# Other places for the staged output projection, eight attention-output buffers, and a shifted plan in block 0

## The chip, the cores and the metric

The kernel runs on one core of one Trainium2 chip. The metric is the device time of one execution in microseconds; lower is better. A program of this kind has five engines: TensorE (PE, whose weight loads are shown as PEld), VectorE (DVE), ScalarE (ACT), GpSimd (POOL) and SyncE (SP). Each works through its own queue in order. TensorE writes its results to PSUM, which has eight banks here; the other engines read them from there into SBUF. DMAs are issued from the queues of SP, ACT and POOL.

## The reference

A token sequence of 2048 rows with 576 columns goes through a layer norm, and the result feeds two branches that are multiplied at the end:

```python
xn = _layernorm(x)
# branch A: attention with 32 query heads on a cache of 16 key/value heads,
#           of which only the last W = 512 positions count
q = (xn @ wq) as 32 heads of 128
p = softmax(q @ k^T * 128 ** -0.5);  o = p @ v
s = concat_heads(o) @ wo                      # 4096 -> 576
# branch B: a token mixer and an MLP
h  = gelu(_layernorm(xn) @ w1)                # 576 -> 576
hs = concat(four column groups of h, shifted by +1, -1, +2, -2 tokens) @ w2
x1 = xn + hs
b  = x1 + gelu(_layernorm(x1) @ w3) @ w4      # 576 -> 4608 -> 576
out = x + s * silu(b)
```

All tensors are bf16.

## The kernel before

**Two stages.** The tokens are cut into four blocks of 512 (`NB` = 4, `TB` = 4 tiles of 128 tokens each). Stage one does branch A for all blocks, with the mixer of branch B woven in; it leaves `s` and `x1` in DRAM (`s_dram`, `x1_dram`). Stage two does the MLP and the final product. Its SBUF pools begin at the place where those of stage one began, so its weights `w3_s`, `w3r_s`, `w4_s` (nine slices of four 128-column chunks, loaded on SP by `load_w`) fall on space that stage one used; each tile waits for the tiles that it covers.

**The loop over heads.** Stage one runs over `U` = 128 heads, 32 per block, and some more steps for the last block's remainder. Step `u` issues on TensorE, in this order: the first quarter of head `u`'s scores (`stage_s`, L403), the query projection of head `u + 1` (`stage_q`, L388), and then the other three quarters of the scores, each followed by a piece of other work: half of head `u - 1`'s product with the values (`stage_v`, L420) after each of the first two, and a third of the step's fill atoms after each of the three. At the end of the step, `stage_t` (L433) issues the transpose of head `u - 1`'s output on SP.

The path of one head: `psq` in PSUM is copied to `qT` (by VectorE at L393 in block 0, by ScalarE at L395 later); scores `sc` become `pT` by an exponential on ScalarE (L405); `po` in PSUM holds two token tiles of output with the row sums in an extra column; VectorE takes the reciprocal (L424) and multiplies into `o` (L425); a DMA transpose on SP turns `o` into `oT`. So a buffer of `o` is held from the first L425 of its head until the transpose has read it. There are four `o` buffers, two `po` banks, three `qT`, ten `pT` and 36 `oT`.

**Work that fills the heads.** Lists give the step at which each other piece is issued: `pe(u, atoms)` for matmuls, which are cut in three parts over the step, and `at(u, fn)` or `later(u, ...)` for the rest. `later` with 3 issues nine steps of a layer norm, three in each head. For a block `b` with `base = 32 * b`, before the change:

- `ln2_steps` from `base + 7`: the second layer norm, into `xnn_b`; `tr2` at `base + 10` to `+13`: four DMA transposes on SP into `xnnT` (L357).
- `b1` (L492): five matmul groups for `w1` from `xnnT`, with the GELU on VectorE and ScalarE (`gelu1`), from `base + 17` in block 0.
- `b2` and `b2_rem` (L543) of the block before, from `base + 21`, whose sum with `xn` goes to an `x1` tile and by SP to `x1_dram` (L570). Its tile is taken one head earlier (`b2_shift`).
- `ln1_steps` for the next block (bn_stats at L133, L134, the inverse root by Newton steps, applied at L144), from head 20 in block 0 and from `base + 24` later; `tr1`: its four transposes on SP into `xT_b` (L357), at heads 23 to 26 in block 0. The next block's `stage_q` reads them.
- `wo_atoms` of the block before: the output projection in five groups, four of 32 wide matmuls (512 columns) and one remainder group of 128 narrow ones (64 columns), at heads `base + 1` to `base + 5`. Each wide group is copied from PSUM by ScalarE (L454), the remainder at L461; then a DMA stores the block to `s_dram` (L462). Block 3's groups come after the last head, and its store is issued by ScalarE; the others by SP.
- Weight loads on GpSimd: `load_wq`, `load_wo`, `load_k`, `load_v`, several of them held back by `late` until a chosen head's `pT` exists.

SP, POOL and PE issue strictly in this written order in stage one. The order on VectorE and ScalarE is made by the framework's scheduler; the instructions under `tc.high_priority` (the copies of `qT` and `kT`, L424, L425, the GELU) are preferred, and the layer norms fill what is left. SP's queue is thus one line in which `stage_t`, `tr1`, `tr2` and the stores stand one behind the other.

**The staging of s, and x1_pool.** Before, `s` is staged in a pool of its own, `so_pool`, with one buffer. `x1_pool` has two buffers, which hold in turn: the staged keys (`load_k`, read last by `prep_k` in head 27), block 0's and block 1's x1, block 0's x1 read back for the MLP (`load_x1(0)`, head 106), and then block 2's and block 3's x1. `w1_sb` is read last by `b1` of block 3, at head 117.

Of the kernel before, what the change touches and what calls it, by code (L numbers as in the profile page):

```python
# [8 lines left out]
P = 128  # L9
# [3 lines left out]
BF16 = mybir.dt.bfloat16  # L13
# [18 lines left out]
def kernel(  # L32
# [18 lines left out]
    _, S, D = A_x.shape  # L51
# [11 lines left out]
    NB = S // QB  # L63
    TB = QB // P
# [31 lines left out]
    def rows(ap, t0, n):  # L96
        return ap[t0 * P:(t0 + n) * P, :].rearrange("(tt p) d -> p tt d", p=P)
# [98 lines left out]
    x1_pool = ctx.enter_context(tc.tile_pool(name="x1_pool", bufs=2))  # L196
# [19 lines left out]
    with ExitStack() as actx:  # L216
        def pool(name, bufs, space=None):
            kw = {} if space is None else {"space": space}
            return actx.enter_context(tc.tile_pool(name=name, bufs=bufs, **kw))
# [7 lines left out]
        w1_sb = res.tile([P, NDC, D], BF16, name="w1_sb")  # L227
# [6 lines left out]
        xraw = pool("xraw", 4)  # L234
        qT_pool = pool("qT_pool", 3)
        pT_pool = pool("pT_pool", 10)
        o_pool = pool("o_pool", 4)
        hb_pool = pool("hb_pool", 2)
        hs_pool = pool("hs_pool", 1)
        g1_pool = pool("g1_pool", 1)  # L240
        so_pool = pool("so_pool", 1)
        oT_pool = pool("oT_pool", 36)
        wo_sb = pool("a_wo", 1).tile([P, Hq, D], BF16, name="wo_sb")

# [8 lines left out]
        def load_x(b, eng):  # L253
            x_t[b] = []
            for tt in range(TB):
                xt = xraw.tile([P, D], BF16, name="xt")
                t = b * TB + tt
                eng.dma_start(out=xt[:], in_=x2[t * P:(t + 1) * P, :])
                x_t[b].append(xt)
# [43 lines left out]
        def late(ap, fn):  # L303
            g = nc.gpsimd.tensor_copy(out=gate[:, :], in_=ap)
            with tc.issue_after(g.ins):
                fn()
# [49 lines left out]
        def transpose_tile(dstT, src, tt):  # L356
            nc.sync.dma_start(out=dstT[:, :, tt * P:(tt + 1) * P], in_=src[:, tt, :], transpose=True)  # L357
# [14 lines left out]
        def tr1(b, tt):  # L372
            transpose_tile(xT_b[b % 2], xn_t[b], tt)
# [62 lines left out]
        so_t = {}  # L436

        def wo_atoms(qb):
            psp, tag = (ps_pq, "pq") if qb == NB - 1 else (ps_wo, "wo")
            groups = []  # L440
            st = {}

            def mm(ps, h, tt, lo, hi):
                nc.tensor.matmul(ps, lhsT=oT_t[qb * Hq + h][:, tt, :], rhs=wo_sb[:, h, lo:hi], start=(h == 0),  # L444
                                 stop=(h == Hq - 1))

            def main(tt, h):
                if tt == 0 and h == 0:
                    so_t[qb] = so_pool.tile([P, TB, D], BF16, name="s_out")
                if h == 0:  # L450
                    st["ps"] = psp.tile([P, M0], FP32, name="pswo", tag=tag)
                mm(st["ps"][:, :], h, tt, 0, M0)
                if h == Hq - 1:
                    nc.scalar.activation(out=so_t[qb][:, tt, 0:M0], in_=st["ps"][:, :], func=ACT.Copy, scale=0.5)  # L454

            def rem(tt, h):
                if tt == 0 and h == 0:
                    st["pr"] = psp.tile([P, TB, R0], FP32, name="pswr", tag=tag)
                mm(st["pr"][:, tt, :], h, tt, M0, D)
                if tt == TB - 1 and h == Hq - 1:  # L460
                    nc.scalar.activation(out=so_t[qb][:, :, M0:D], in_=st["pr"][:, :, :], func=ACT.Copy, scale=0.5)  # L461
                    (nc.scalar if qb == NB - 1 else nc.sync).dma_start(out=rows(s_dram, qb * TB, TB),  # L462
                                                                       in_=so_t.pop(qb)[:])

            for tt in range(TB):
                groups.append([lambda tt=tt, h=h: main(tt, h) for h in range(Hq)])
            groups.append([lambda tt=tt, h=h: rem(tt, h) for tt in range(TB) for h in range(Hq)])
            return groups

# [3 lines left out]
        def ln2_steps(b):  # L473
            return layernorm_steps(small, [xnn_b[:, tt, 0:D] for tt in range(TB)],
                                   [xn_t[b][:, tt, 0:D] for tt in range(TB)])

        def tr2(b, tt):
            transpose_tile(xnnT, xnn_b, tt)

        def b1(b, c):  # L480
            st = {}

            def mm(kc):
                if kc == 0:
                    if c == 0:
                        hb_t[b] = hb_pool.tile([P, 5, QB + 2 * PAD], BF16, name="hb")
                        if b == 0:
                            nc.vector.memset(hb_t[b][:, :, 0:PAD], 0.0)
                        if b == NB - 1:
                            nc.vector.memset(hb_t[b][:, :, PAD + QB:], 0.0)  # L490
                    st["ph"] = ps_pq.tile([P, QB], FP32, name="ph", tag="pq")
                nc.tensor.matmul(st["ph"][:, :], rhs=xnnT[:, kc, :],  # L492
                                 lhsT=w1r_sb[:, kc, :] if c == 4 else w1_sb[:, kc, c * c4:c * c4 + P],
                                 start=(kc == 0), stop=(kc == NDC - 1))
                if kc == NDC - 1:
                    gelu1(b, c, st["ph"])

            return [lambda kc=kc: mm(kc) for kc in range(NDC)]
# [25 lines left out]
        def b2_shift(b):  # L524
            with tc.high_priority(offset=HP):
                b2_shift_(b)
# [18 lines left out]
        def b2(b, tt):  # L545
            st = {}

            def mm(c):
                if c == 0:
                    st["ps"] = ps_wo.tile([P, M0], FP32, name="psx1", tag="wo")  # L550
                b2_mm(st["ps"][:, :], b, tt, c, 0, M0)
                if c == 4:
                    with tc.high_priority(offset=HP):
                        nc.vector.tensor_tensor(out=x1o_t[b][:, tt, 0:M0], in0=st["ps"][:, :],
                                                in1=xn_t[b][:, tt, 0:M0], op=ALU.add)

            return [lambda c=c: mm(c) for c in range(5)]
# [38 lines left out]
        def at(u, fn):  # L596
            fill.setdefault(u, []).append(fn)

        def pe(u, atoms):
            pe_fill.setdefault(u, []).extend(atoms)  # L600
# [5 lines left out]
        def later(u, make, per):  # L606
            cell = []
            for i in range(2 * TB + 1):
                def step(i=i):
                    if not cell:  # L610
                        cell.append(make())
                    cell[0][i]()
                at(u + i // per, step)

        for b in range(NB):
            base = b * Hq
            if b > 0:
                for i, group in enumerate(wo_atoms(b - 1)):
                    pe(base + 1 + i, group)
            later(base + 7, lambda b=b: ln2_steps(b), 3)  # L620
            for tt in range(TB):
                at(base + 10 + tt, lambda b=b, tt=tt: tr2(b, tt))
            for c in range(5):
                pe(base + (15 if 0 < b < NB - 1 else 17) + c, b1(b, c))
            for bb in ([b - 1] if b > 0 else []) + ([b] if b == NB - 1 else []):
                o2 = base + (28 if bb == b else 23 if b == NB - 1 else 21)
                at(o2 - 1, lambda bb=bb: b2_shift(bb))
                for tt in range(TB):
                    pe(o2 + tt, b2(bb, tt))
                pe(o2 + 3, b2_rem(bb))  # L630
            if b + 1 < NB:
                at(base + (8 if b == 0 else 4), lambda b=b: late(pT_t[b * Hq + (8 if b == 0 else 4)][0][0:1, 0:1],
                                                                 lambda: load_x(b + 1, nc.gpsimd)))
                u1 = base + (24 if b else 20)
                later(u1, lambda b=b: ln1_steps(b + 1), 3)
                for tt in range(TB):
                    at(u1 + (3 + tt // 2 if b else 3 + tt), lambda b=b, tt=tt: tr1(b + 1, tt))
        for i, group in enumerate(wo_atoms(NB - 1)):
            pe(U + 1 + i, group)
        at(2, lambda: late(pT_t[2][0][0:1, 0:1], load_w1))  # L640
# [59 lines left out]
    with ExitStack() as bctx:  # L700
# [181 lines left out]
        with tc.manual_schedule(engines={PE, DVE, ACTE}):  # L882
# [7 lines left out]
            for d in range(0, ND, 2):  # L890
                b = d // NP
# [4 lines left out]
                if end:  # L896
                    assert not work
                    bs = bs_pool.tile([P, TB, D], FP32, name="bs")
                    x1 = x1_t[b]
# [48 lines left out]
            b = NB - 1  # L948
# [34 lines left out]
            tt = TB - 1  # L983
# [11 lines left out]
    with tc.If(flag > 0):  # L995
        with ExitStack() as gctx:
# [19 lines left out]
            with tc.For_i(0, NT, 1) as t:  # L1016
# [10 lines left out]
                for h in range(Hq):  # L1027
                    g = h // REP
                    if h % REP == 0:
                        k_nat = work.tile([P, KCH, Dh], BF16, name="r_k")  # L1030
                        nc.sync.dma_start(out=k_nat[:],
                                          in_=A_k_cache[0, g, K0:, :].rearrange("(kc p) d -> p kc d", p=P))
                        v_g = work.tile([P, KCH, Dh], BF16, name="r_v")
                        nc.sync.dma_start(out=v_g[:],
                                          in_=A_v_cache[0, g, K0:, :].rearrange("(kc p) d -> p kc d", p=P))
# [80 lines left out]
```

## Time and profile before

| what | value |
|---|---|
| median of nine runs | 849.03 us (846.96 to 850.35) |
| the profiled execution | 855.24 us, span 853.5 us |
| mean granted clock of TensorE | 0.994 |
| TensorE matmuls | 829.3 us busy, 97% of the span, 7896 instructions |
| ScalarE | 461.0 us, 54% |
| VectorE | 426.7 us, 50% |
| GpSimd | 76.8 us, 9% |
| exponentials, L405 | 290.3 us, 512 of 596 ns |
| products with the values, L420 | 162.3 us, 2048 of 221 ns |
| output projection, wide, L444 | 114.2 us, 379 ns each |
| multiplications into `o`, L425 | 107.9 us, 256 of 422 ns |

Times in the lines of a profile are from the start of the span. Matmuls are pipelined, so the sum of their durations is more than the time that they take one after another. "Idle before" is the time that an engine did nothing before a group of instructions; the releaser is what ended that idle time. In the second part of the page each digit is the busy share of one fortieth of the span, in tenths; the row PEclk is the clock that TensorE was granted. In the timeline a line shows the start, the time from there to the end of the group, the engine, the line in the kernel, the operation, what it writes and reads, the count, and in brackets the idle time ahead of it. Stage one ends near 563 us, where the first matmuls of the MLP (L769) start.

### The profile page before, as it was taken

How to read it: one execution, taken by the hardware profiler on the slowest of the kernel's cores; microseconds unless marked ns; L12 is line 12 of the kernel's file. 1: busy time of each engine (PE TensorE's matmuls, PEld its weight loads, DVE VectorE, ACT ScalarE, POOL GpSimd, SP SyncE). 2: the span in 40 equal slices, each digit the busy share in tenths (PEclk: the TensorE clock that was granted, in tenths of full speed). 3: DMA queues.
4: the chain of work that ended last, by engine and by line, in shares of the span. 5: the costliest groups of instructions: out<-in, count | busy, mean ns of one | idle time of the engine just before them, and what ended most of it. 6: DMA issues, size and time to landing. Idle time of an engine off the chain costs nothing.

```text
span 853.5 us, 19361 instructions
## 1 busy us (share of the span) xinstructions
PE 829.3 (97%) x7896; PEld 487.4 (57%) x7980; DVE 426.7 (50%) x1351; ACT 461.0 (54%) x825; POOL 76.8 (9%) x134
## 2 busy tenths in 40 slices
PE   7997989999999999999999999999999999999996
PEld 5664655566565566565466566455555555555555
DVE  4785951166772155773135786024236636655434
ACT  4774773388885378876359876032333424334610
POOL 2532100310010101100001000000000000000000
PEclk9998999999999999999999999999999999999999
DMA  6998591254355137345128425995001321230101
GB/s 170 207 233 147 125 159 48 72 124 100 87 123 88 47 82 131 67 128 89 41 72 134 94 65 110 243 330 146 2 2 43 53 78 43 37 94 15 44 15 45
DMA packets 139983, 83.94 MB, mean 98 GB/s; under 512 B 106944, under 2 KB 133248, under 8 KB 139888
## 3 DMA queue, kind: packets, MB, share of 16 engines
q1 hardware_dynamic: 130048, 53.01, 31.0%
q0 software_dynamic: 8448, 28.15, 12.1%
q8 instruction: 64, 1.05, 0.5%
q10 hardware_dynamic: 1392, 1.48, 0.5%
q14 instruction: 31, 0.25, 0.1%
HBM read 49.17 MB, written 9.44 MB: 69 GB/s over the span
## 4 chain that ended last, share of the span: by engine, by line


## 5 line engine op out<-in xcount | busy, mean ns | idle before, releaser
L405 ACT ACTIVATE pT<-sc 128x512 bf16<-128x512 f32 x512 | 290.3, 596 | 110.8 <-PE sc L403 98.8
L403 PE MATMUL sc<-qT,kT 128*128 128x512 bf16 x493 | 175.4, 379 | 1.3 <-DVE qT L393 0.6
L420 PEld LDWEIGHTS <-pT 128*128 128x128 bf16 x2048 | 140.2, 98 | 58.7 <-DVE o L425 8.1
L420 PE MATMUL po<-v_sb,pT 128*128 128x129 bf16 x2048 | 162.3, 221 | 8.4 <-DVE o L425 7.2
L388 PE MATMUL psq<-xT_b,wq_b 128*128 128x512 bf16 x603 | 151.9, 379 | 2.8 <-DMA xT_b<-xn_b 0.7
L424 DVE RECIPROCAL ri_b<-po 128x2 f32<-128x2 f32 x256 | 43.1, 169 | 190.5 <-PE po L420 186.6
L769 PE MATMUL ph<-xT_b,w_s 64*128 64x512 bf16 x976 | 127.1, 376 | 0.0
L806 PE MATMUL pm<-w_s,h 64*128 64x512 bf16 x864 | 122.3, 377 | 0.0
L425 DVE TENSOR_TENSOR o<-po,ri_b 128x256 bf16<-128x256 f32 x256 | 107.9, 422 | 17.7 <-DMA oT<-o 11.3
L444 PE MATMUL pswo<-wo_sb,oT 128*128 128x512 bf16 x497 | 114.2, 379 | 0.8
L787 ACT ACTIVATE h<-ph 128x512 bf16<-128x512 f32 x67 | 39.4, 597 | 130.4 <-PE ph L769 130.4
L388 PEld LDWEIGHTS <-wq_b 128*128 128x128 bf16 x640 | 62.4, 98 | 74.7 <-issue 2.7
L806 PEld LDWEIGHTS <-h 64*128 64x128 bf16 x1728 | 70.8, 94 | 55.6 <-issue 0.4
L444 PEld LDWEIGHTS <-oT 128*128 128x128 bf16 x1024 | 65.0, 98 | 55.1 <-DMA oT<-o 0.2
L806 PE MATMUL pr<-w_s,h 64*128 64x64 bf16 x864 | 90.2, 189 | 0.2 <-ACT h L787 0.2
L769 PEld LDWEIGHTS <-w_s 64*128 64x128 bf16 x1152 | 57.2, 94 | 48.3 <-issue 0.2
L395 ACT ACTIVATE qT<-psq 128x512 bf16<-128x512 f32 x96 | 57.4, 598 | 28.4 <-PE psq L388 27.0
L785 DVE COPY hx<-ph 128x512 f32<-128x512 f32 x55 | 38.0, 691 | 69.3 <-PE ph L769 69.3
L403 PEld LDWEIGHTS <-kT 128*128 128x128 bf16 x512 | 47.5, 98 | 28.7 <-DVE qT L393 1.2
L265 POOL DMA_DIRECT2D wq_b<-in_A_wq_dram x30 | 23.4, 780 | 315.4 <-PE psq L388 296.2
L787 ACT ACTIVATE h<-hx 128x512 bf16<-128x512 f32 x55 | 34.7, 630 | 8.0 <-DVE hx L785 6.0
L759 DVE TENSOR_SCALAR fence<-ph,ph 1x1 f32<-1x1 f32 x61 | 12.8, 209 | 50.0 <-PE ph L769 49.4
(122 smaller groups left out, 646.5 us busy)
## 6 DMA issues: line engine op xcount, KB each, us to landing
wq_b<-in_A_wq_dram POOLq DMA_DIRECT2D x30, 512.0 KB, 5.1
w_s<-in_B_w_dram SPq DMA_DIRECT2D x9, 576.0 KB, 7.0
wo_sb<-in_A_wo_dram POOLq DMA_DIRECT2D x8, 576.0 KB, 5.5
w_s<-in_B_w_dram SPq DMA_DIRECT2D x9, 512.0 KB, 7.8
x_dram<-x SPq DMA_DIRECT2D x4, 576.0 KB, 3.5
x<-x_dram SPq DMA_DIRECT2D x4, 576.0 KB, 5.3
s_b<-s_dram SPq DMA_DIRECT2D x4, 576.0 KB, 5.2
x_b<-in_A_x_dram SPq DMA_DIRECT2D x4, 576.0 KB, 6.0
```

Of the source, the lines that this page charges most:

```text
L388: nc.tensor.matmul(psq[:, :], lhsT=w[:, kc, hh * Dh:(hh + 1) * Dh], rhs=xT_b[qb % 2][:, kc, :], start=(kc == 0), stop=(kc == NDC - 1))
L395: nc.scalar.activation(out=qT[:, :], in_=psq[:, :], func=ACT.Copy)
L403: nc.tensor.matmul(sc[:, :], lhsT=kT[:, g, kc * P:(kc + 1) * P], rhs=qT_t[u][:, :], start=True, stop=True)
L405: nc.scalar.activation(out=pT[:, :], in_=sc[:, :], func=ACT.Exp, scale=SCALE)
L420: nc.tensor.matmul(po[:, j, :], lhsT=pTs[kc][:, tt * P:(tt + 1) * P], rhs=v_sb[:, g, kc, 0:Dh + 1], start=(kc == 0), stop=(kc == KCH - 1))
L424: nc.vector.reciprocal(out=ri, in_=po[:, :, Dh])
L425: nc.vector.tensor_tensor(out=o[:, t0:t0 + 2, :], in0=po[:, :, 0:Dh], in1=ri.unsqueeze(2).to_broadcast([P, 2, Dh]), op=ALU.mult)
L444: nc.tensor.matmul(ps, lhsT=oT_t[qb * Hq + h][:, tt, :], rhs=wo_sb[:, h, lo:hi], start=(h == 0), stop=(h == Hq - 1))
L769: nc.tensor.matmul(ps[i][:, :], lhsT=lhsT, rhs=xT[half, kc, :], start=first, stop=last, skip_group_check=True)
L785: nc.vector.tensor_copy(out=src[:, :], in_=ps[i][:, :])
L787: nc.scalar.activation(out=h3[:, :], in_=src[:, :], func=ACT.Gelu_apprx_tanh)
L806: nc.tensor.matmul(out, lhsT=h3_t[b, fc][half, tt * P:(tt + 1) * P], rhs=w4_s[fc // WS][half, fc % WS, lo:hi], start=key not in started, s ...
```

## The change

The pool `so_pool` is gone. Blocks 0 to 2 stage `s` in a tile of `x1_pool`, block 3 in the first four rows of `w1_sb`. `o_pool` has eight buffers in place of four. Block 0's output projection is issued at heads 34 to 38 in place of 33 to 37; those of blocks 1 and 2 keep their heads. In block 0, the first layer norm for block 1 is issued from head 19 in place of 20, and its four transposes `tr1` at heads 24 to 27 in place of 23 to 26.

```diff
-        o_pool = pool("o_pool", 4)
+        o_pool = pool("o_pool", 8)
         hb_pool = pool("hb_pool", 2)
         hs_pool = pool("hs_pool", 1)
         g1_pool = pool("g1_pool", 1)
-        so_pool = pool("so_pool", 1)
         oT_pool = pool("oT_pool", 36)
...
                 if tt == 0 and h == 0:
-                    so_t[qb] = so_pool.tile([P, TB, D], BF16, name="s_out")
+                    so_t[qb] = w1_sb[:, 0:TB, :] if qb == NB - 1 else x1_pool.tile([P, TB, D], BF16, name="x1")
...
                     (nc.scalar if qb == NB - 1 else nc.sync).dma_start(out=rows(s_dram, qb * TB, TB),
-                                                                       in_=so_t.pop(qb)[:])
+                                                                       in_=so_t.pop(qb)[:, :, :])
...
                 for i, group in enumerate(wo_atoms(b - 1)):
-                    pe(base + 1 + i, group)
+                    pe(base + (2 if b == 1 else 1) + i, group)
...
-                u1 = base + (24 if b else 20)
+                u1 = base + (24 if b else 19)
                 later(u1, lambda b=b: ln1_steps(b + 1), 3)
                 for tt in range(TB):
-                    at(u1 + (3 + tt // 2 if b else 3 + tt), lambda b=b, tt=tt: tr1(b + 1, tt))
+                    at(u1 + (3 + tt // 2 if b else 5 + tt), lambda b=b, tt=tt: tr1(b + 1, tt))
```

## The prediction

> **What bounds the kernel now.** I read the page first. Its first part puts TensorE at 97% of the span, and the slices of its second part show where the rest lies.
>
> ```profile
> PE 829.3 (97%) x7896; PEld 487.4 (57%) x7980; DVE 426.7 (50%) x1351; ACT 461.0 (54%) x825; POOL 76.8 (9%) x134
> PE   7997989999999999999999999999999999999996
> PEclk9998999999999999999999999999999999999999
> ```
>
> One slice is 21.3 us. Apart from the fill and the tail, TensorE has holes in the fourth slice (with a lower clock) and in the sixth. Everything else runs at its own pace, so only those holes, or new ones, can move the time. The view of waits, asked for TensorE and then VectorE, names them (total us, times, longest):
>
> ```profile
> PE po L420 <- DVE o L425: 7.2, 2, 4.5
> ```
> ```profile
> DVE o L425 <- DMA oT<-o: 11.3, 3, 6.2
> ```
>
> Twice TensorE waits for a bank of `po` which VectorE hasn't emptied, because the `o` buffer it must write is still being read by an old transpose. The view by windows sizes both holes (length, then busy time of PE, PEld, DVE, ACT, POOL, then clock, DMA share, GB/s):
>
> ```profile
> 65.00:70.00 5.00, 1.33 (x7) 0.39 (x4) 0.00 (x0) 1.54 (x3) 0.82 (x2) 0.85 1.08 143
> 70.00:75.00 5.00, 4.20 (x22) 2.62 (x23) 2.63 (x8) 0.60 (x1) 0.00 (x0) 0.50 1.23 236
> 75.00:80.00 5.00, 4.95 (x37) 2.93 (x37) 4.40 (x14) 3.40 (x6) 0.00 (x0) 0.96 0.66 64
> 110.00:115.00 5.00, 2.25 (x18) 1.13 (x17) 0.88 (x4) 1.89 (x4) 0.00 (x0) 1.00 1.25 135
> ```
>
> Mean clocks of 0.85 and 0.96 mean that it was halved from about 68.5 (5 x 0.15 / 0.5 = 1.5 us of that window) to 75.4. In the second hole it stays whole. The timeline of PE gives the order at the first hole, which decides what comes next:
>
> ```profile
> 65.95 0.38 PE L403 MATMUL sc<-qT,kT 128*128 128x512 bf16 x1
> 70.80 1.05 PE L420 MATMUL po<-v_sb,pT 128*128 128x129 bf16 x8 [4.47 <-DVE o L425]
> 71.64 0.63 PE L492 MATMUL ph<-xnnT,w_sb 128*128 128x512 bf16 x1
> ```
>
> Last, the narrow view of one transpose, the fourth of `xnnT`, which that L492 matmul reads:
>
> ```profile
> L357 SPq DMA_TRANSPOSE xnnT<-xnn_b x1: 1662/1662/1662, 58.2 to 58.2; - x1
> ...
> DMA to landing us min/median/max: 12.4/12.4/12.4
> ```
>
> It was issued at 58.2 and landed at 70.6, in the same jam of transposes behind the weight loads (DMA share above 1) as head 11's `oT`, which held the `o` buffer (issued 55.5, 14.7 us, landed 70.2).
>
> **The change part by part.**
>
> *Eight `o` buffers, first hole.* Head 15 no longer waits for head 11, so the eight L420 matmuls run straight after the `sc` matmul, from 66.17. At full clock eight take 0.47 us (77.16 to 77.63 in the timeline), so TensorE reaches L492 at 66.64. There it needs all of `xnnT`, at 70.6 plus the 0.1 us that VectorE took to start after head 11's landing: 70.7. The old wait is thus replaced by a new one of 4.06 us; nothing in the change starts those transposes earlier. What is won depends on the clock. Before, 70.80 to 75.4 ran at half clock: 2.3 us of full-speed work. If the clock falls as before, 70.7 to 75.4 gives 2.35, plus the 0.47 already done: a gain of 0.5. If it stays whole: 4.7 + 0.47 - 2.3 = 2.9. Of the idle times seen, 2.69 us kept the clock and 4.47 us lost it. 4.06 lies nearer to the second; between the two gains in proportion, 0.5 + 2.4 x (4.47 - 4.06) / (4.47 - 2.69) = 1.05. I take 1.0 and keep 0.5 and 2.9 as ends.
>
> [...]
>
> *Eight buffers and the earlier LN1, second hole.* SP's queue stood at `tr1` for block 1 from 98.4 until the first L144 apply ended at 107.2; behind it head 22's transpose went out at 108.5 and landed 5.5 us later, at 114.0, and head 26's `o` waited for it. With eight buffers only head 30 would need that one, so the 2.69 us vanish as a wait for `o`. Next late is `xT_b`: L388 for head 32 (at 122.0 before) needs the fourth `tr1`. Before, the four `tr1` and the transposes between took 107.2 to 115.7, and the last landed 2.6 us later: 11.1 us after the apply. Now `tr1` starts a head later, but LN1 is given out a head earlier (a light head is 2.88 us: 116.26 to 122.02 for two). If the apply doesn't move, it lands at 118.3 and is needed at 122.0 - 2.7 - 1.0 = 118.3: just in time. If it comes earlier, there is slack. I take 2.7 whole. If the extra head of `tr1` all comes on top, the wait is 2.9 - 0.5, and some 0.3 is left.
>
> *LN1's steps themselves.* Eight L133, four L134, four L144 (3.42 + 0.80 + 1.60 us) and eleven small ones near 0.16: 7.6 us of VectorE, unchanged in number. VectorE is busy 9.07 of 10 us at 75 to 85 and 9.97 at 85 to 95, beside the GELU of block 0. TensorE doesn't stall there now: two `po` banks hide it. Taken at 0; priced below as a rival.
>
> *Block 0's wo one head later.* The same 128 wide and 128 narrow L444 matmuls, and the L454 and L461 copies (0.60 and 0.38 us) with them: no time by themselves, since TensorE is full on both sides. `oT` has 36 buffers; head 36's transpose needs head 0's, free only in the remainder group, which is now in head 38. So on SP the transposes of heads 36 and 37 stand for one more filled head, with the `s` store (before at 174.1) in between, and four or five `o` buffers fill up behind them. Eight cover this; with four it would cost up to a light head, 2.9 us. On POOL nothing moves past anything. Zero.
>
> *Output projection of blocks 0 to 2 in `x1` slots.* Same copies and stores, other addresses. The `k` tiles there are read last at head 27 (110.4), and the copy comes at head 34. The `s` store landed 3.4 us after 174.1, while block 0's x1 takes its slot at head 51 or later. Zero. If a slot were held, ACT would wait at L454 with the L405 exponentials behind it, and the `po` matmuls after those.
>
> *Block 3's in `w1_sb`.* By the sizes in the listing `w1_sb` lies 48.4 to 54.1 KB into the stage's space; of the MLP's weight slices, 9.2 KB each from the same start, the sixth (46.1 to 55.3 KB) covers it. Its loads now wait for the `s` store: issued on ACT at 563.9, landing 3.4 (the fastest such store) to 8.6 us later (that one), so 567.3 to 572.5 instead of an issue at 556.7. On SP, slices seven to nine, then the `s` and `x` loads, stand behind. Slice six landed at 565.6; it will at 576 to 581. It is first read by the eleventh pair of up matmuls, at 599.2 (pairs start every 3.93 us), so some 18 us cover it. The next slices are needed every 7.9 us and arrive every 3.6. Block 1's `xT_b` (SP, 585.5) is needed only by pair 19, near 631. Zero.
>
> *Sum.* 1.0 + 2.7 = 3.7 us. The profiled execution took 855.24 us with a span of 853.5, so 851.5 would be expected of it. The nine runs have a median of 849.03, 6.2 us less; I carry the 3.7 us over: 845.3.
>
> **The rivals.**
>
> *The waits only change hands.* The first hole becomes the wait for `xnnT` with the clock lost (0.5), the second a wait of L388 for `xT_b` (0.3). For it: 70.6, and no slack at 118.3. Against: LN1 starts earlier, and the clock may hold. 849.0 - 0.8 = 848.2.
>
> *Slower: LN1 ahead of urgent work on VectorE.* If its 7.6 us, less the 0.9 us idle at 75 to 85, all stand before `qT` and `o` in that in-order queue, TensorE loses 6.7: 845.3 + 6.7 = 852.0. From 3.7 us it cancels the gain. Against: LN1's steps lie singly between urgent ones now.
>
> *Slower: the weights wait from their first slice*, if the space is laid out otherwise than I worked out. The first slice would land about 8.8 us (as it did) after 567.3, against a start at 563.4: 12.7 us, 858.0. It decides from the first slice that is held; five clear ones suffice.
>
> **How the numbers follow.** My forecast has 0.60 (gains of 2.0 to 5.6: 843.4 to 847.0), the waits changing hands 0.22, VectorE 0.13, the weights 0.05. Less than about 0.2% (1.7 us) can't be told from no change here, so faster 0.60, same 0.22, slower 0.18. The range goes from 843.0 through the second case to 851.5, which leaves out the weights, the worst of VectorE and little below: under 2 in 10.
>
> **What would show it.** Right: no wait of `o` for a transpose; a new PE wait for `xnnT` of about 4 us at L492 near 70.7; no hole at 110 to 115; SP's weight loads broken off before the sixth slice until the `s` store lands, with no PE wait at L769. Wrong: L492 starting near 66.7, or the old hole still there; a PE wait for `xT_b` near 118; PE waits for `qT` or `o` at 78 to 100; any L769 wait for weights.

## The result, and the profile after

The changed kernel takes 861.04 us (median of ten runs), against 849.03 before: a ratio of 1.0135, with a 95% interval of 1.0111 to 1.0159. The change costs some 12 us where I had forecast a gain of 3.7. Here and below, medians are of all runs of a kernel, while ratios leave out runs more than 1.5% above the kernel's fastest. Its profiled execution took 857.53 us with a span of 855.8.

The page of the changed kernel, second part (busy tenths and clock in forty slices of the span):

```profile
PE   7999999999999999999999999769999999999996
PEclk9999999999999999999999999979999999999998
```

The two holes in the fourth and sixth slices are gone, and so is the dip of the clock there. A new hole lies in the 26th and 27th slices, with a dip of the clock in the 27th, where stage one hands over to the MLP. The view of waits names it, for TensorE and then for SP's queue (total us, times, longest):

```profile
PE ph L768 <- DMA w_s<-in_B_w_dram: 11.5, 1, 11.5
```
```profile
SPq L737 <- PE pswr L443: 27.9, 1, 27.9
```

The first matmul of the MLP waits 11.5 us for its weights. On SP, the load of `s_b` (L737, which the MLP needs only at the end of its first block) waits 27.9 us for the last matmul of the output projection. The timeline of SP shows why the second wait makes the first. Before:

```profile
531.72 3.02 SPq L433 DMA_TRANSPOSE oT<-o  x2
534.85 0.52 SPq L204 DMA_DIRECT2D x<-x_dram  x1
535.46 0.46 SPq L723 DMA_DIRECT2D w_s<-in_B_w_dram  x1
```

and after:

```profile
519.57 3.02 SPq L432 DMA_TRANSPOSE oT<-o  x2
522.69 0.52 SPq L204 DMA_DIRECT2D x<-x_dram  x1
551.37 0.36 SPq L737 DMA_DIRECT2D s_b<-s_dram  x1
551.78 0.50 SPq L739 DMA_DIRECT2D x_b<-in_A_x_dram  x1
552.33 0.58 SPq L737 DMA_DIRECT2D s_b<-s_dram  x1
552.96 1.38 SPq L722 DMA_DIRECT2D w_s<-in_B_w_dram  x1
```

The weights used to follow the last transposes at once, while the output projection of block 3 still had some 28 us to go. Now three loads of the MLP's later data stand ahead of them in the same queue, and the first of these can't go before the output projection's last matmul, most likely because it takes space that the projection reads to its end; the trace does not name the space. So no weight is issued before 552.96, and the first one lands 9.9 us later, when TensorE has long run dry. The view by windows sizes it (length, then PE, PEld, DVE, ACT and POOL busy, then clock, DMA share, GB/s):

```profile
555.00:560.00 5.00, 0.00 (x0) 0.00 (x0) 0.00 (x0) 0.00 (x0) 0.00 (x0) 0.50 1.09 389
560.00:565.00 5.00, 2.12 (x12) 0.73 (x14) 0.00 (x0) 0.00 (x0) 0.00 (x0) 0.50 1.11 332
565.00:570.00 5.00, 5.00 (x36) 2.03 (x34) 1.11 (x3) 2.65 (x4) 0.00 (x0) 0.72 1.11 319
```

From 555 to 560 all engines stand still while the weights arrive. The mean of 0.72 in the last window says that the clock came back 5 x 0.28 / 0.5 = 2.8 us into it, at 567.8. TensorE began again at 562.88, so it worked 4.9 us at half clock and lost 2.45 more: 11.54 + 2.45 = 14.0 us in all.

In stage one the waits for `o` are gone, as forecast. VectorE's writes into `o` no longer wait for a transpose (busy and mean, then the idle time ahead of them):

```profile
L424 DVE TENSOR_TENSOR o<-po,ri_b 128x256 bf16<-128x256 f32 x256 | 108.0, 422 | 6.5 <-DVE ri_b L423 0.3
```

Before, that idle time was 17.7 us, 11.3 of it ended by `oT<-o`. The place of the first hole in the timeline of PE after:

```profile
63.97 0.38 PE L402 MATMUL sc<-qT,kT 128*128 128x512 bf16 x1
64.18 0.63 PE L419 MATMUL po<-v_sb,pT 128*128 128x129 bf16 x8
64.65 0.81 PE L491 MATMUL ph<-xnnT,w_sb 128*128 128x512 bf16 x3
```

There is no wait here at all, not even the one for `xnnT` that I had expected: in this execution its fourth transpose landed 7.3 us after its issue at 54.7, at 62.0. The length of this jam is not fixed: in the profile of the kernel before the same transpose took 12.4 us to land, and in that of the run with `xn_b[1]` below, whose block 0 is the same as here, TensorE waits 14.9 us for `xnnT`. That fits the two profiled executions being only 2.3 us apart where the medians are 12.0 apart: the one before, with a long jam, lies 6.2 us above its median, and the one after, with none, 3.5 us below its own.

### The profile page after: what moved, and what is told of

The parts are those of the page before. It is cut to its first block, busy times and chain, and to the rows that moved or that the text cites. A ratio compares the mean times of both kernels' runs of the same rounds, so it can differ in the third digit from the quotient of the medians.

```text
span 855.8 us, 19360 instructions
## 1 busy us (share of the span) xinstructions
PE 827.6 (97%) x7896; PEld 485.0 (57%) x7980; DVE 427.7 (50%) x1351; ACT 461.1 (54%) x825; POOL 76.8 (9%) x134
## 4 chain that ended last, share of the span: by engine, by line
## 5 line engine op out<-in xcount | busy, mean ns | idle before, releaser
L387 PE MATMUL psq<-xT_b,wq_b 128*128 128x512 bf16 x604 | 152.4, 379 | 2.5 <-DMA xT_b<-xn_b 0.4
L768 PE MATMUL ph<-xT_b,w_s 64*128 64x512 bf16 x976 | 128.3, 379 | 11.7 <-DMA w_s<-in_B_w_dram 11.5
L387 PEld LDWEIGHTS <-wq_b 128*128 128x128 bf16 x640 | 62.4, 98 | 74.5 <-issue 2.2
L768 PEld LDWEIGHTS <-w_s 64*128 64x128 bf16 x1152 | 57.7, 95 | 61.7 <-DMA w_s<-in_B_w_dram 11.7
```

The lines of the kernel that those rows point to most:

```text
L387: nc.tensor.matmul(psq[:, :], lhsT=w[:, kc, hh * Dh:(hh + 1) * Dh], rhs=xT_b[qb % 2][:, kc, :], start=(kc == 0), stop=(kc == NDC - 1))
L768: nc.tensor.matmul(ps[i][:, :], lhsT=lhsT, rhs=xT[half, kc, :], start=first, stop=last, skip_group_check=True)
```

## The experiments

Four questions were asked in turn: is the loss the use of `w1_sb`, is it the order on SP or the space, what makes that order, and which parts of the rest gain anything.

**The changed kernel without `w1_sb`.**

```diff
-                    so_t[qb] = w1_sb[:, 0:TB, :] if qb == NB - 1 else x1_pool.tile([P, TB, D], BF16, name="x1")
+                    so_t[qb] = xn_b[1][:, :, 0:D] if qb == NB - 1 else x1_pool.tile([P, TB, D], BF16, name="x1")
```

> The changed kernel, with block 3's output projection staged in xn_b[1] (free since block 3's mixer, and not part of the space that the MLP's weights take) in place of w1_sb; all else as changed. Theory A (the use of w1_sb moves the s and x loads ahead of the weights on SP): the 11.5 us wait of the first L768 matmul and its half-clock stretch of 13.7 us go, the first weight slice is issued right after the last transpose; 861 less about 14, so 846 to 848, and a little faster than before. Theory B (the eight buffers or the shifted heads cost the time in runs without a profile): it stays at 858 to 861.

Measured: 846.16 us, ratio to before 0.9927 (0.9894 to 0.9960). 861.04 - 846.16 = 14.9 us go with this one line (by the two ratios some 17), against the 14.0 counted in the trace. What is left of the change is faster than before. Four of its 13 runs took 858 to 862 us, though; the profiled one is among them, and in it TensorE waits 14.9 us for `xnnT` at L491. So eight buffers don't end the long jam, they only take the wait for `o` out of it.

**The kernel before with only the use of `w1_sb`.**

```diff
-                    so_t[qb] = so_pool.tile([P, TB, D], BF16, name="s_out")
+                    so_t[qb] = w1_sb[:, 0:TB, :] if qb == NB - 1 else so_pool.tile([P, TB, D], BF16, name="s_out")
```

> The kernel before, with only block 3's output projection staged in w1_sb; blocks 0 to 2 keep so_pool, four o buffers, heads as before. Theory A: the whole loss comes with this one edit, plus what the rest of the change wins: 860 to 864, a wait of 11 to 12 us of the MLP's first matmul for its weights, clock halved around it. Theory B: no change from 849.

Measured: 868.23 us, ratio 1.0250 (1.0199 to 1.0302). The view of waits of PE in this run:

```profile
PE ph L769 <- DMA w_s<-in_B_w_dram: 11.4, 1, 11.4
PE po L420 <- DVE o L425: 2.5, 1, 2.5
```

The one edit makes the whole loss; the second hole of the kernel before is still there, since the buffers and heads are. The median lies a few us above what I expected. Its four runs spread from 863.9 to 874.5, and I did not settle why.

**The changed kernel with the order on SP put right.** `w1_sb` is used as in the change; only the `s` and `x` loads must follow the last weight load, the last one of `w4_s`, which is kept in `last_w[0]`.

```diff
-        load_sx(0)
+        with tc.issue_after(last_w[0].ins):
+            load_sx(0)
         load_x1(1)
```

> The changed kernel, w1_sb staging included, with the first s and x loads made to stand behind the last weight load on SP (issue_after). Theory A, that it is the order on SP and not the space: 846 to 848 as with xn_b[1]; the first five slices are issued from the last transpose on, the sixth only after the store of s, without a wait at L768. Rival A2, that the weights themselves must wait for w1_sb's last reader: the wait of the first matmul stays, 858 to 861.

Measured: 843.89 us, ratio 0.9944 (0.9923 to 0.9964), with no wait for weights. It is the order, not the space. But the queue did not run as expected. The view of waits of SP, and SP's timeline:

```profile
SPq L729 <- DMA s_dram<-w_sb: 23.1, 1, 23.1
```
```profile
533.65 0.53 SPq L724 DMA_DIRECT2D w_s<-in_B_w_dram  x1
534.22 1.87 SPq L728 DMA_DIRECT2D w3r_s<-in_B_w_dram  x2
559.87 0.38 SPq L729 DMA_DIRECT2D w_s<-in_B_w_dram  x1
```

SP stood for 23 us at the second slice's `w4_s` already, not at the sixth, until the store of `s` had landed. The slice and a half before that were enough to start the MLP, and the rest came in time. Why that load waits for that store, the trace does not tell. It need not be the space: in the run with `xn_b[1]`, which isn't under the weights, a `w4_s` load also waited for the store of `s`.

```profile
SPq L727 <- DMA s_dram<-xn_b: 1.2, 1, 1.2
```

**What makes the order: pools.** First `w1_sb` in a pool of its own, which may also move it:

```diff
-        w1_sb = res.tile([P, NDC, D], BF16, name="w1_sb")
+        w1_sb = pool("a_w1", 1).tile([P, NDC, D], BF16, name="w1_sb")
```

> The changed kernel with w1_sb in a pool of its own, at the place that it had in the run with pools for each slice, but all nine weight slices in one pool as before. Theory A3 (the plan holds a whole new pool until the last reader of any space under it): the s load stands before all weights on SP, waits some 28 us for the last output projection matmul, and the first L768 matmul waits 11 to 12 us; 857 to 861. Rival A4 (the place of w1_sb decides): weights first, as in the run with pools for each slice.

Measured: 858.88 us, ratio 1.0108 (1.0028 to 1.0187); L768 waits 11.4 us and `s_b` again stands ahead of the weights on SP, for 28.4 us. These are two runs only, made after those with the pools below. Then, with that pool kept, each weight slice in a pool of its own:

```diff
-        res = pool("b_res", 1)
...
         for i in range(NSL):
+            res = pool(f"b_res{i}", 1)
             w3_s.append(res.tile([P, NF, WS * P], BF16, name=f"w3_s{i}"))
```

> The changed kernel, w1_sb staging included, but w1_sb allocated in a pool of its own at its old place and each slice of the MLP's weights in a pool of its own. Theory A3 (the scheduler plans the reuse of space by whole pools: the new pool of all slices waits in the plan for the old pool's last reader, which the change made the store of s, so the s and x loads look ready first and are put ahead): now only the slice that covers w1_sb is held, the other slices stand first on SP, no wait of several us at L768, 843 to 847. Rival A4 (the order turns on the place of w1_sb alone): the wait of 11 to 12 us stays, 858 to 862.

Measured: 857.41 us, ratio 1.0081 (1.0048 to 1.0114). (`w1_sb` is allocated by the same line as in the run above, so it need not lie at its old place, as the expectation has it.) The order came out as theory A3 says: the first weight went out at 522.68, straight after the transposes. The time did not follow, for a new reason. The waits of PE and DVE, and SP's timeline:

```profile
PE ph L768 <- DVE hx L784: 11.8, 2, 11.5
```
```profile
DVE ln_st L159 <- DMA x<-x_dram: 13.5, 1, 13.5
```
```profile
555.55 0.49 SPq L737 DMA_DIRECT2D s_b<-s_dram  x1
559.87 0.37 SPq L722 DMA_DIRECT2D w_s<-in_B_w_dram  x1
...
563.60 0.51 SPq L204 DMA_DIRECT2D x<-x_dram  x1
```

Eight slices go out one after another; only the ninth is held: SP stands there from 556.04 to 559.87, most likely for the store of `s`. Whether `w1_sb` lies under the ninth, the trace does not show. Now the read-back of block 1's x1 (L204) stands behind the held slice, at 563.60 in place of 522.69. The layer norm for block 1 sits on VectorE ahead of the copies that free TensorE's banks, waits 13.5 us for it, and TensorE waits with it. Putting this load first gives the third run with these pools:

```diff
-        nc.sync.dma_start(out=x1[:], in_=rows(x1_dram, b * TB, TB))
+        last_x1[0] = nc.sync.dma_start(out=x1[:], in_=rows(x1_dram, b * TB, TB))
...
+        load_x1(1)
-        with tc.issue_after(last_t[0].ins):
+        with tc.issue_after(last_t[0].ins), tc.issue_after(last_x1[0].ins):
             for i in range(NSL):
                 load_w(i)
...
         load_sx(0)
-        load_x1(1)
```

> As the run with pools of their own for w1_sb and each weight slice, but the read-back of block 1's x1 stands on SP ahead of the weights, as in the kernel before. If the 11.55 us hole of that run came only from that load standing behind the held slice: no hole at the start of the MLP, 842 to 847. If the held slice or the s and x loads behind it cost by themselves: a wait at L768 for w_s stays, 850 or more.

Measured: 843.95 us, ratio 0.9932 (0.9906 to 0.9957), without a hole at the MLP's start. In these three kernels the same line allocates `w1_sb`. With one pool for all slices the weights stood behind `s_b`; with a pool for each slice eight of the nine did not. So the place of `w1_sb` alone (rival A4) does not make the order, and theory A3 forecast the order in both cases. How the scheduler plans, by whole pools or otherwise, is my guess all the same: the plan is not in the traces. What they show is that the first slice had nothing to wait for: it went out 0.1 us after the issue of the read-back ahead of it, at 524.99 in this run and at 528.22 in the run with the order on SP pinned.

**Parts of the gain.** Eight buffers and the other staging (with `xn_b[1]`), LN1, its transposes and wo at the heads before:

```diff
-                    pe(base + (2 if b == 1 else 1) + i, group)
+                    pe(base + 1 + i, group)
-                u1 = base + (24 if b else 19)
+                u1 = base + (24 if b else 20)
-                    at(u1 + (3 + tt // 2 if b else 5 + tt), lambda b=b, tt=tt: tr1(b + 1, tt))
+                    at(u1 + (3 + tt // 2 if b else 3 + tt), lambda b=b, tt=tt: tr1(b + 1, tt))
```

> As the run with xn_b[1], but LN1, its transposes and block 0's output projection at the heads that they had before: eight o buffers and the other staging alone. If the buffers alone end both holes: 846 to 847, the same as with the shifted heads. If the shift of LN1 and its transposes matters: 1 to 3 us slower than with it, by a wait for xT_b or a hole near 110.

Measured: 844.19 us, ratio 0.9964 (0.9926 to 1.0002). There is no hole near 110, since TensorE nowhere waits for `o`; its longest wait for a transpose is this one:

```profile
PE ph L491 <- DMA xnnT<-xnn_b: 0.9, 1, 0.9
```

The buffers alone end the second hole, and the shifted heads add nothing that these runs can tell. The interval just reaches no change, so the gain of this run by itself is not shown. The shifted heads alone, in the kernel before (the same three lines the other way round, four buffers, `so_pool`):

> The kernel before, with only the shifted heads: LN1 from 19, its transposes at 24 to 27, block 0's wo at 34 to 38; four o buffers, so_pool kept. If the shift ends the second hole by itself (SP does not stand long before the LN1 transposes): no wait for o near 110, 846 to 847; the first hole is then held by o or by xnnT as before. If only the buffers end it: a wait of 2 to 3 us for o near 110 stays, 849 to 850. With oT's 36 buffers held a head longer and four o buffers, up to 2.9 us more near 170.

Measured: 849.86 us, ratio 0.9982 (0.9944 to 1.0020): no change. In its profile, one with a long jam, the second hole has shrunk to 0.4 us (9.8 us in two waits for `o`, the longest 9.4), so the shift seems to end it nearly by itself, but the four buffers keep the first hole: TensorE waits 9.4 us for `o` there, then 4.1 us for `xnnT`. The staging alone (the buffers put back to four in the kernel with eight):

> The staging alone: blocks 0 to 2 in x1_pool slots, block 3 in xn_b[1]; four o buffers, heads as before, no so_pool. The staging in x1 slots is free: 849 to 850, the same holes as before near 66 and 110, and no wait at L768.

Measured: 849.85 us, ratio 0.9986 (0.9948 to 1.0024): no cost that these runs can tell, with the second hole (2.6 us) as before, in a profile with a long jam too (6.1 and 5.0 us).

**Three attempts on the first hole.** With eight buffers and the heads of before, the wo loads moved out of the jam:

```diff
-            at(4 + 3 * i, lambda i=i: late(pT_t[4 + 3 * i][0][0:1, 0:1], lambda: load_wo(i)))
+            at(15 + 2 * i, lambda i=i: late(pT_t[15 + 2 * i][0][0:1, 0:1], lambda: load_wo(i)))
```

> Eight o buffers, block 3's s staged in xn_b[1], heads as before, and the eight loads of wo issued at heads 15, 17, ... 29 in place of 4, 7, ... 25, out of the stretch in which the transposes of xnnT jam. Theory C (the first hole is the wait of L491 for xnnT behind weight loads, and varies from run to run with the jam): the fourth xnnT transpose lands before 62, no wait at L491, no runs of 850 and more, 841 to 843. Rival (the jam is made by the transposes themselves or by wq, k and v): L491 still waits 1 to 4 us, 843 to 846, with slow runs among them.

Measured: 850.40 us, ratio 1.0000 (0.9966 to 1.0034): the gain of the buffers is lost again. `xnnT` was early enough, but now the next transposes, which `stage_q` reads, came late. That the jam moved there with the loads is the likely reason; the run does not show what delayed them:

```profile
PE psq L387 <- DMA xT_b<-xn_b: 2.9, 2, 2.7
```

Or block 0's `b1` two heads later, so that TensorE has other work while `xnnT` is late, with the shifted heads and then with those of before:

```diff
-                pe(base + (15 if 0 < b < NB - 1 else 17) + c, b1(b, c))
+                pe(base + (15 if 0 < b < NB - 1 else 17 if b else 19) + c, b1(b, c))
```

> The changed kernel with block 3's s in xn_b[1], and block 0's mixer matmuls (b1) two heads later, at 19 to 23, so that TensorE has 5.8 us more of heads to do while xnnT's transposes wait behind the weight loads. Theory C (the first hole is L491's wait for xnnT): a wait of up to 5.8 us goes, and the clock stays whole; the median falls to 841 to 842.5 and the runs lie closer. Rival: VectorE, on which the GELU now meets LN1, becomes late, and with it the transposes of xT_b for block 1: a wait of L387 near 115, 845 to 848.

> The same with LN1, its transposes and block 0's wo at the heads of the kernel before. Theory C: 841 to 842.5. If the shift of LN1 matters once the GELU comes later: a wait for xT_b, 1 to 3 us slower than with the shifted heads.

Measured: 845.83 us, ratio 0.9942 (0.9905 to 0.9979), and 850.59 us, ratio 1.0007 (0.9975 to 1.0039). L491 no longer waited for `xnnT`, but L387 did, for `xT_b`: 4.3 us in the profile of the first and 4.8 in that of the second. The first can't be told from leaving `b1` where it was, and the second is worse. Here the shifted heads do matter: without them this kernel is 4.8 us slower on the same chip, more than the 1 to 3 us expected.

## Why the prediction was right or wrong

*Block 3's in `w1_sb`: wrong, and the whole miss.* The step that failed is the sentence that on SP, slices seven to nine, then the `s` and `x` loads, stand behind the sixth slice. I took the order in which the loads are written for the order on SP. That holds in stage one, which is scheduled by hand. In stage two it does not: two loads of `s_b` and one of `x_b`, written after all nine slices, went out ahead of the first one, from 551.37 on. That the scheduler put all nine off because the change lengthened the life of a tile under their pool is theory A3; it forecast the order of the two runs with pools, but no trace holds the plan. The first weight went out at 552.96 and not near 523, right after the last transposes, and the 18 us of cover that I counted were for loads that stood behind it. The rival "the weights wait from their first slice" had the right victim and nearly the right price (12.7; the wait is 11.54 us and the half clock after it, which I left out, another 2.45). The price agrees by luck: I had the weights wait for the store of `s` to land (3.4 us) and then 8.8 us for the first slice; in fact three loads stood ahead for 1.6 us from the last matmul of stage one at 551.34, and the first slice took 9.9 us. I had only thought of another layout as its cause, which made it look improbable. That the sixth slice is the one over `w1_sb` is neither shown nor disproved: in no run with `w1_sb` did SP break off just before the sixth.

*Eight buffers, first hole: mechanism right, size not a constant.* `o` waits for no transpose in any profile with eight buffers, and L491's wait for `xnnT` is what comes next. My 4.06 us was one execution's jam; the profiled runs with eight buffers and `b1` at its old heads show from none (the changed kernel) over 0.9 to 3.3 us (the run with the order put right), apart from the long jam told of above. In the changed kernel one of my signs of being wrong came out: L491 started without a wait.

*Second hole: right.* It is gone in the changed kernel, the buffers alone end it, and `xT_b` is indeed next. I had called it just in time; in the profile of the changed kernel, the fourth `tr1` was issued at 106.5 and landed 2.6 us later, 1.0 us before L387 for head 32 at 110.11. The three attempts above fall into exactly that wait.

*LN1, wo one head later, the `x1` slots, each at nothing: right as far as these runs can tell.* The staging alone can't be told from before (0.9948 to 1.0024), and the kernel with the heads of before can't be told from the one with the shifted heads. With `b1` two heads later that no longer holds.

*The sum of stage one: right, in part by luck.* Without `w1_sb` the change measures 0.9927 (0.9894 to 0.9960), so 3.4 to 9.0 us of 849.03; the medians on that chip are 3.9 apart. I had put 3.7, of which the first hole's 1.0 was worked out from the length of one jam, which the runs show not to be fixed (no wait for `xnnT` in the changed kernel, 14.9 us in the run with `xn_b[1]`).

*The rival on VectorE: not seen.* In the profile of the changed kernel TensorE had no wait for `qT` or `o` at 78 to 100.

## What to carry to other kernels

Before an idle tile is given a new use, ask what space it shares a pool with and who inherits that space: here the new use of one tile came with three loads ahead of all nine weight slices, and the 27.9 us that SP stood at the first of them became 11.5 us of TensorE waiting for weights. Where an order on a queue matters, pin it, and check each load in it that something reads early (here the weights, then the x1 read-back). Moving the loads out of a transpose jam did not pay here (850.40 us), since the next transposes came late in their turn (2.9 us of waits for `xT_b`); so look who reads those. The kernels to keep are the change with `xn_b[1]` as block 3's staging, or with the order on SP pinned: 843.9 to 846.2 us, which these runs cannot rank. Nor do they settle whether the long jam, which I take to be behind the four times of 858 to 862 us among 13 runs of the first, comes less often in the second, where none of 12 runs took more than 848.34.

## What the runs showed of the hardware that I had not expected

The clock does not follow the length of an idle time alone. In the kernel before, 2.69 us of idling for `o`, up to 114.57, left it whole: the windows from 110 to 115 and from 115 to 120 both show 1.00. In the run with only `w1_sb` changed, it fell with the 2.5 us for `o`, as its windows show:

```profile
105.00:110.00 5.00, 2.99 (x20) 2.17 (x20) 2.93 (x9) 0.92 (x3) 0.00 (x0) 0.70 0.73 146
110.00:115.00 5.00, 5.00 (x41) 3.03 (x40) 2.52 (x7) 3.59 (x7) 0.58 (x1) 0.96 0.45 86
```

If it fell to half, the 0.50 that the windows from 70 to 75 of the kernel before and from 555 to 560 of the changed kernel show, that is 3.0 us of half clock in the first and 0.4 in the second, 3.4 in all. So reading the price of a wait off one shorter and one longer idle time, as I did, has no ground. What else decides it, no run here shows.
